# An attention plus mixture-of-experts kernel: expert work in 640-slot blocks with 320-column matmuls, deep gathers, unordered row scatters and a dynamic loop for overflow

## The chip, the cores and the metric

The kernel runs on one core of a Trainium2 chip. The metric is device time in microseconds (us) of one execution; runs of one kernel are summed up by their median. The profile shows one execution, taken by the hardware profiler; its times count from the first instruction. A core has TensorE (PE in the profile; PEld is its weight load), VectorE (DVE), ScalarE (ACT), GpSimd (POOL) and SyncE (SP). SP and POOL also issue transfers; those of POOL go through the software queue q0, those of SP through q1.

## What is computed

Eight batches of eight heads of attention over 576 positions (head width 64) with a position bias made by a small two-layer network; the result, 4608 rows of 512, then passes through a two-layer ReLU network whose weights are chosen by each row's domain:

```python
scores = scale * np.matmul(q, k.transpose(0, 1, 3, 2)) + bias   # bias: position network, per head
attn = softmax(scores); x = np.matmul(attn, v)                  # x: 4608 rows of 512
for e in range(8):
    mask = domain_id == e
    h = np.maximum(x[mask] @ w1[e], 0.0)                        # 512 -> 1024
    out[mask] = h @ w2[e]                                       # 1024 -> 512
```

`domain_id` is drawn at random with a fixed seed. The eight experts get 566, 557, 545, 612, 562, 561, 618 and 587 rows.

## The kernel before

The kernel is written in a tile framework: the author writes operations in program order, and a scheduler at compile time lays them out per engine, taking on each engine the earliest operation of the program that it expects to be ready. Each engine then executes its list strictly in order and waits where an input or a buffer is not there yet. Buffers come from pools; a pool opened after another was closed lies on the same memory, so its first use waits for the last use of the older one. The size of a buffer ring is `bufs`.

The stages, in program order:

1. `_setup_constants` and `_phase_fire` (L47 to L141) build the position bias; `biasall` goes through one long exp on ACT (L141). The buffers of `_phase_fire` (pool `fsb`) are free when its last matmul (L133) is done.
2. `_phase_route` (L144 to L221) gives each row a slot: expert e owns slots 768 e to 768 e + 767 (`CAP` = 768, `NCH` = 6 tiles of 128 slots). DVE computes the position of each row (`posi`, L196), and 36 indirect scatters issued by POOL (L203), each of 128 row numbers, write them into `fire_perm` in device memory, which was filled with -1. All 36 write the same tensor, so each waits for the one before it. Then SP reads the table back (L208), and DVE replaces empty slots by the slot of the same lane in the expert's first tile, giving `gidx` (L221). An empty slot thus repeats a real row.
3. `_phase_attention` (L224 to L320) runs over the batches. POOL loads q and k of a batch with a cast to float16 (L234, L237; ring of 4); per head TensorE transposes them (L247, L250), multiplies (L287), ACT takes the exp (L291, 24 per batch) into `eT` (ring of 8, one per head), DVE multiplies by the bias (L297). SP loads values (L259, L261; ring of 2), POOL casts them into `vext` (L262 to L266; ring of 8). When all heads are there, TensorE multiplies by the values (L308), DVE normalises (L313, L314), and SP stores rows of `fire_x` (L320).
4. `_phase_moe` (L323 to L363) runs over the experts; for each it loads both weight matrices (L329, L332, on POOL with a cast; ring of 2), then for each of 6 tiles of 128 slots: gathers 128 rows of `fire_x` (L336, POOL; ring of 2), transposes them with four TensorE operations (L341), copies to SBUF on DVE (L344), multiplies by w1 in 32 matmuls with 128 columns (L348), applies ReLU on ACT (L353), multiplies by w2 in 8 matmuls with 512 columns (L356), copies the result to SBUF (L359, DVE; ring of 2) and scatters its rows to the output (L360, POOL). All 48 scatters write the output tensor, so each waits for the one before. The pool `msb` of this stage lies on the memory of attention, so its first load (L329) waits for the last store of `fire_x`.

Of the kernel before, what the change touches and what calls it, by code (L numbers as in the profile page):

```python
# [16 lines left out]
P = 128  # L17
# [8 lines left out]
CAP = 768  # L26
NCH = CAP // 128
NTOK = B * S

# [114 lines left out]
def _phase_route(tc, G, moe_domain_id):  # L144
    nc = tc.nc
    perm_dram = nc.dram_tensor("fire_perm", (E * CAP, 1), I32, kind="Internal").ap()
# [18 lines left out]
    ut = pbuf.tile([P, P], F16, tag="ut", name="ut")  # L165
    nc.gpsimd.memset(ut, 1.0)
    nc.gpsimd.affine_select(out=ut, in_=ut, compare_op=AO.is_ge, fill=0.0,
                            base=-1, channel_multiplier=-1, pattern=[[1, P]])
    apref = pbuf.tile([P, 8, 1], F32, tag="apref", name="apref")
    with tc.tile_pool(name="pps", bufs=1, space=bass.MemoryType.PSUM) as pps:  # L170
        app = pps.tile([P, 8], F32, tag="app", name="app")
        nc.tensor.matmul(out=app, lhsT=ut, rhs=rowtot16, start=True, stop=True)
        nc.vector.tensor_copy(out=apref, in_=app.unsqueeze(-1))
    pa = pbuf.tile([P, 8, 80], F32, tag="pa", name="pa")
# [5 lines left out]
    for sh in (1, 2, 4, 8, 16, 32):  # L180
# [6 lines left out]
    etile = pbuf.tile([P, 8, 36], F32, tag="etile", name="etile")  # L187
    nc.vector.tensor_scalar(out=etile, in0=rap(eif, 0, [[1, 8], [0, 36]]),
                            scalar1=float(CAP), scalar2=None, op0=AO.mult)
    nc.vector.tensor_tensor(out=rtile, in0=rtile, in1=etile, op=AO.add)  # L190
# [6 lines left out]
    neg48 = pbuf.tile([P, 48], I32, tag="neg48", name="neg48")  # L197
    nc.gpsimd.memset(neg48, -1)
    nc.sync.dma_start(out=perm_dram.rearrange("(p c) o -> p (c o)", c=48), in_=neg48)
    nidx = pbuf.tile([P, 36], I32, tag="nidx", name="nidx")  # L200
    nc.gpsimd.iota(nidx, base=0, channel_multiplier=1, pattern=[[128, 36]])
    for c in range(36):
        nc.gpsimd.indirect_dma_start(  # L203
            out=perm_dram[:, :],
            out_offset=bass.IndirectOffsetOnAxis(ap=posi[:, c:c + 1], axis=0),
            in_=nidx[:, c:c + 1], in_offset=None)
    permE = pbuf.tile([P, E * NCH, 1], I32, tag="permE", name="permE")
    nc.sync.dma_start(out=permE, in_=bass.AP(tensor=perm_dram.tensor, offset=0,  # L208
                                             ap=[[1, 128], [128, E * NCH], [1, 1]]))
    permEf = pbuf.tile([P, E, NCH], F32, tag="permEf", name="permEf")  # L210
    nc.vector.tensor_copy(out=permEf, in_=permE.rearrange("p (e kk) o -> p e (kk o)", e=E))
    mneg = pbuf.tile([P, E, NCH], F32, tag="mneg", name="mneg")
    nc.vector.tensor_scalar(out=mneg, in0=permEf, scalar1=0.0, scalar2=-1.0,
                            op0=AO.min, op1=AO.mult)
    tsel = pbuf.tile([P, E, NCH], F32, tag="tsel", name="tsel")
    nc.vector.tensor_tensor(out=tsel, in0=permEf[:, :, 0:1].to_broadcast([P, E, NCH]),
                            in1=mneg, op=AO.mult)
    nc.vector.tensor_tensor(out=tsel, in0=tsel, in1=mneg, op=AO.add)
    nc.vector.tensor_tensor(out=permEf, in0=permEf, in1=tsel, op=AO.add)
    G.gidx = pbuf.tile([P, E, NCH], I32, tag="gidx", name="gidx")  # L220
    nc.vector.tensor_copy(out=G.gidx, in_=permEf)  # L221
# [100 lines left out]

def _phase_moe(tc, G, moe_w1, moe_w2, x_dram, out):  # L323
    nc = tc.nc
    with tc.tile_pool(name="msb", bufs=1) as msb, \
         tc.tile_pool(name="mps", bufs=1, space=bass.MemoryType.PSUM) as mps:
        for e in range(E):
            w1e = msb.tile([P, 4, FF], F16, tag="w1e", name="w1e", bufs=2)
            nc.gpsimd.dma_start(out=w1e,  # L329
                                in_=moe_w1[e].rearrange("(dc dl) f -> dl dc f", dl=128))  # L330
            w2e = msb.tile([P, 8, DM], F16, tag="w2e", name="w2e", bufs=2)
            nc.gpsimd.dma_start(out=w2e,  # L332
                                in_=moe_w2[e].rearrange("(fc fl) d2 -> fl fc d2", fl=128))
            for kk in range(NCH):
                xg = msb.tile([P, DM], F16, tag="xg", name="xg", bufs=2)
                nc.gpsimd.indirect_dma_start(  # L336
                    out=xg[:], out_offset=None, in_=x_dram[:],
                    in_offset=bass.IndirectOffsetOnAxis(ap=G.gidx[:, e, kk: kk + 1], axis=0))
                pxt = mps.tile([P, 4, 128], F16, tag="pxt", name="pxt", bufs=2)
                for dc in range(4):  # L340
                    nc.tensor.transpose(out=pxt[:, dc, :],  # L341
                                        in_=xg[:, 128 * dc: 128 * dc + 128], identity=G.idn)
                xgT = msb.tile([P, 4, 128], F16, tag="xgT", name="xgT", bufs=2)
                nc.vector.tensor_copy(out=xgT, in_=pxt)  # L344
                hps = mps.tile([P, FF], F32, tag="hps", name="hps", bufs=2)
                for fc in range(8):
                    for dc in range(4):
                        nc.tensor.matmul(out=hps[:, 128 * fc: 128 * fc + 128],  # L348
# [72 lines left out]
```

## Time and profile before

| what | value |
|---|---|
| runs | 908.75, 915.71, 915.02 us; median 915.02 us |
| span of the profiled execution (its total is not given separately) | 900.5 us |
| granted TensorE clock, mean | 0.935 |
| bias and routing arithmetic | 0 to about 285 us |
| attention | about 285 to 631 us |
| experts | about 632 to 900 us |

The span runs from the first to the last instruction; the measured time of a run also holds what lies before and after. In a row of the timeline stand the start, the duration, the engine, the line and operation, what it writes and reads, how many were merged into the row, and in brackets how long the engine had been idle and what ended that. In a row of waits stand who waited for whom, the total, the number of waits and the longest. In a row of a group stand the total busy time, the mean duration of one in ns, and the idle time of the engine in front of them.

### The profile page before, as it was taken

The page shows a single profiled execution, that of the slowest core. Times are in us where ns is not written, and L with a number is a line of the kernel's source. Part 1 is how long each engine was busy: PE and PEld are TensorE (multiplying, and loading weights), DVE is VectorE, ACT ScalarE, POOL GpSimd, SP SyncE. Part 2 cuts the span into 40 slices and gives each one's busy share as a digit, 9 for nine tenths or more (in the row PEclk, how much of TensorE's full clock was granted, in tenths as well). Part 3 has the DMA queues.
Part 4 walks back from the last instruction along what each step waited for, and adds up shares of the span by engine and source line. Part 5 has one row for each costly group of instructions (what it writes and reads, how often), then busy time and mean ns, then how long its engine had stood idle before and what let it go on. Part 6 is the DMA issues. An engine that isn't in the chain of part 4 may idle for free.

```text
span 900.5 us, 15948 instructions
## 1 busy us (share of the span) xinstructions
PE 573.2 (64%) x6513; PEld 377.7 (42%) x6513; DVE 570.0 (63%) x1106; ACT 259.0 (29%) x279; POOL 290.8 (32%) x547
## 2 busy tenths in 40 slices
PE   0132555555553387786858778786287977887785
PEld 0011233333332245454536555454265655555563
DVE  5989999999999286766758796886021211121121
ACT  0021200000001973535545383754021211211111
POOL 7821100000001735654523243030343453343451
PEclk9999999999999998969879997999599998999999
DMA  1000000000002968389393949020947647736721
GB/s 3 1 5 1 0 1 1 1 1 0 1 1 28 123 55 74 49 99 72 75 59 76 91 59 104 22 61 25 171 125 153 144 120 159 164 98 149 158 99 60
DMA packets 150233, 60.52 MB, mean 67 GB/s; under 512 B 128656, under 2 KB 141456, under 8 KB 150160
## 3 DMA queue, kind: packets, MB, share of 16 engines
q0 software_dynamic: 93824, 45.12, 38.0%
q1 hardware_dynamic: 56336, 14.39, 7.6%
q8 instruction: 51, 0.84, 0.4%
q14 instruction: 22, 0.18, 0.1%
HBM read 68.35 MB, written 17.34 MB: 95 GB/s over the span
## 4 chain that ended last, share of the span: by engine, by line
DVE 31%; DMA 24%; PE 20%; issue 10%; ACT 10%; POOL 4%; POOLq 0%; SPq 0%; DVEq 0%; ACTq 0%
DVE biasall L140 10%; DMA out_dram<-res,gidx 10%; ACT eT L291 8%; DVE hrelu L126 8%; PE sc L287 5%; PE ops L356 5%; DMA fire_x<-xt 4%; PE hps L348 3%; DMA xg<-fire_x,gidx 3%; DMA fire_perm<-nidx,posi 3%; PE hpre L119 3%; PE pu L308 3%; DVE eT L297 3%; DVE WBIG L77 2%; DMA bm<-in_w_dram 2%
## 5 line engine op out<-in xcount | busy, mean ns | idle before, releaser
L291 ACT ACTIVATE eT<-sc 128x1152 f16<-128x1152 f32 (+1 forms) x192 | 172.3, 965 | 138.3 <-PE sc L287 104.2
L359 DVE COPY res<-ops 128x512 f32<-128x512 f32 x48 | 33.2, 692 | 189.7 <-PE ops L356 127.9
L297 DVE TENSOR_TENSOR eT<-eT,biasall 128x576 f16<-128x576 f16 (+1 forms) x320 | 132.1, 459 | 23.9 <-ACT eT L291 22.5
L119 PE MATMUL hpre<-Tnat,WBIG 128*128 128x512 f16 (+1 forms) x288 | 91.7, 422 | 80.9 <-DVE Tnat L99 40.0
L287 PE MATMUL sc<-qkT 128*128 128x512 f16 (+5 forms) x640 | 117.0, 311 | 36.0 <-DVE qkT L255 17.3
L126 DVE TENSOR_SCALAR hrelu<-hpre,b1x 128x576 f16<-128x576 f32 x144 | 113.6, 818 | 2.4 <-PE hpre L119 2.1
L353 ACT ACTIVATE hsb<-hps 128x1024 f16<-128x1024 f32 x48 | 49.1, 1023 | 223.2 <-PE hps L348 192.6
L356 PE MATMUL ops<-w2e,hsb 128*128 128x512 f16 x384 | 98.5, 403 | 17.7 <-ACT hsb L353 9.5
L133 PE MATMUL eb<-W2BIG,hrelu 128*128 128x32 f16 (+1 forms) x720 | 55.0, 197 | 81.6 <-DVE biasall L140 71.8
L348 PE MATMUL hps<-xgT,w1e 128*128 128x128 f16 x1536 | 101.0, 223 | 6.0 <-DVE xgT L344 5.5
L348 PEld LDWEIGHTS <-w1e 128*128 128x128 f16 x1536 | 95.4, 100 | 21.2 <-issue 11.0
L140 DVE CAST biasall<-eb 128x512 f16<-128x512 f32 (+1 forms) x45 | 104.2, 2595 | 0.0
L308 PE MATMUL pu<-vext,eT 128*128 128x65 f16 (+1 forms) x1600 | 77.8, 211 | 27.1 <-DVE xt L314 18.7
L133 PEld LDWEIGHTS <-hrelu 128*128 128x128 f16 (+1 forms) x720 | 46.3, 126 | 110.2 <-issue 91.2
L360 POOL DMA_INDIRECT out_dram<-res,gidx x48 | 47.4, 988 | 131.3 <-DMA out_dram<-res,gidx 71.5
L308 PEld LDWEIGHTS <-eT 128*128 128x128 f16 (+1 forms) x1600 | 68.4, 112 | 39.4 <-DVE xt L314 26.4
L287 PEld LDWEIGHTS <-qkT 128*128 128x128 f16 (+1 forms) x640 | 51.0, 105 | 66.8 <-issue 23.9
L119 PEld LDWEIGHTS <-WBIG 128*128 128x128 f16 x288 | 28.6, 106 | 109.5 <-issue 55.3
L356 PEld LDWEIGHTS <-hsb 128*128 128x128 f16 x384 | 35.7, 102 | 63.3 <-issue 16.7
L231 POOL MEMSET qkT<- 64x1152 f16 x2 | 2.0, 1052 | 180.8 <-PE eb L133 180.8
L262 POOL CAST vext<-vf 128x256 f16<-128x256 f32 x64 | 29.7, 465 | 80.2 <-PE pu L308 64.2
L336 POOL DMA_INDIRECT xg<-fire_x,gidx x48 | 46.8, 975 | 24.7 <-issue 12.9
(78 smaller groups left out, 612.6 us busy)
## 6 DMA issues: line engine op xcount, KB each, us to landing
vf<-in_v_dram SPq DMA_DIRECT2D x64, 128.0 KB
w1e<-in_moe_w_dram POOLq DMA_DIRECT2D x8, 1024.0 KB
w2e<-in_moe_w_dram POOLq DMA_DIRECT2D x8, 1024.0 KB
q<-in_q_dram POOLq DMA_DIRECT2D x8, 576.0 KB
k<-in_k_dram POOLq DMA_DIRECT2D x8, 576.0 KB
fire_x<-xt SPq DMA_DIRECT2D x32, 128.0 KB
vf<-in_v_dram SPq DMA_DIRECT2D x64, 16.0 KB
xg<-fire_x,gidx POOLq DMA_INDIRECT x48
```

The source lines that it names most:

```text
L119: nc.tensor.matmul(out=hp[:, js: js + jwd], lhsT=G.WBIG[:, m, :], rhs=G.Tnat[:, blk, js: js + jwd], start=True, stop=True,)
L126: nc.vector.tensor_scalar(out=hr, in0=hp, scalar1=G.b1x4[:], scalar2=0.0, op0=AO.add, op1=AO.max)
L133: nc.tensor.matmul(out=eb[0:jw, 32 * k16: 32 * k16 + 32], lhsT=hrl[k16][:, j0: j0 + jw], rhs=G.W2BIG[:, 0:32], start=True, stop=True,)
L140: nc.vector.tensor_copy(out=oap, in_=eb[0:jw, :])
L287: nc.tensor.matmul(out=po, lhsT=qkT[:, 1, j0: j0 + jw], rhs=qkT[:, 0, i0s: i0s + iwd], start=True, stop=True)
L291: nc.scalar.activation(out=eT[0:jw0, jgl: jgl + njc, :], in_=sc[0:jw0, 0:njc, :], func=AF.Exp, bias=0.0, scale=scale)
L297: nc.vector.tensor_tensor(out=eT[0:jw, jcn, :], in0=eT[0:jw, jcn, :], in1=G.biasall[0:jw, jcn, h, :], op=AO.mult)
L308: nc.tensor.matmul(out=pu[0:icw, hq, 0:65], lhsT=eTs[h][:, jcn, ic0: ic0 + icw], rhs=vexts[h][:, jcn, 0:65], start=(jcn == 0), stop=(jcn = ...
L348: nc.tensor.matmul(out=hps[:, 128 * fc: 128 * fc + 128], lhsT=w1e[:, dc, 128 * fc: 128 * fc + 128], rhs=xgT[:, dc, :], start=(dc == 0), st ...
L353: nc.scalar.activation(out=hsb, in_=hps, func=AF.Relu, bias=0.0, scale=1.0)
L356: nc.tensor.matmul(out=ops_, lhsT=hsb[:, fc, :], rhs=w2e[:, fc, :], start=(fc == 0), stop=(fc == 7))
L360: nc.gpsimd.indirect_dma_start(out=out[:], out_offset=bass.IndirectOffsetOnAxis(ap=G.gidx[:, e, kk: kk + 1], axis=0), in_=res[:], in_offse ...
```

## The change

- `CAP` goes from 768 to 640, so an expert has 5 tiles. Rows beyond 640 of an expert go to overflow tiles of 128 slots (`NOVF` = 38 of them at most) behind the fixed slots. The routing counts rows per expert with a second small matmul, derives how many overflow tiles there are and which expert each belongs to, and adds an offset to the slots of such rows. This is some 20 more small operations on DVE.
- Empty slots hold `PAD`. The gather index turns them into row 0; the scatter index keeps them, and the scatter skips rows out of bounds.
- The 36 slot scatters and all output scatters are declared free of order among each other (`_no_order`).
- The expert stage works by blocks: five gathers and transposes into `xT`, then the first product over all 640 slots in 8 chunks of two halves with 320 columns (64 matmuls for 160), ReLU per chunk on ACT, then the second product tile by tile. `xg` has a ring of 6, `res` of 4.
- Expert 0's weights are loaded ahead of attention into a pool of their own (`wsb`), which lies between the long-lived pools and attention's, on memory that `_phase_fire` used. Even experts use `wsb`, odd ones `msb`.
- After the last expert a dynamic loop runs once per overflow tile; its count is read from SBUF at run time.

The core of the diff (the arithmetic of the overflow offsets is cut):

```diff
-CAP = 768
+CAP = 640
...
+NOVF = 38
+NSLOT = E * CAP + 128 * NOVF
+PAD = 1 << 20
...
-    ut = pbuf.tile([P, P], F16, tag="ut", name="ut")
+    ut = pbuf.tile([P, 2, P], F16, tag="ut", name="ut")
...
+        for t in range(2):
+            nc.tensor.matmul(out=app[:, t, :], lhsT=ut[:, t, :], rhs=rowtot16, start=True, stop=True)
...
+    cnt = apref[:, 1, :, :]
...
     for c in range(36):
-        nc.gpsimd.indirect_dma_start(
-            out=perm_dram[:, :],
+        _no_order(tc, "slots", nc.gpsimd.indirect_dma_start(
+            out=G.perm_dram[:, :],
             out_offset=bass.IndirectOffsetOnAxis(ap=posi[:, c:c + 1], axis=0),
-            in_=nidx[:, c:c + 1], in_offset=None)
...
+            in_=nidx[:, c:c + 1], in_offset=None))
+    G.sidx = pbuf.tile([P, E * NCH, 1], I32, tag="sidx", name="sidx")
+    nc.sync.dma_start(out=G.sidx, in_=bass.AP(tensor=G.perm_dram.tensor, offset=0,
+                                              ap=[[1, 128], [128, E * NCH], [1, 1]]))
...
+    _pad_to_zero(nc, pbuf, G.gidx, G.sidx, [P, E * NCH, 1], "g")
...
+def _pad_to_zero(nc, pool, out, idx, shape, tag):
+    f = pool.tile(shape, F32, tag="pzf" + tag, name="pzf" + tag)
+    nc.vector.tensor_copy(out=f, in_=idx)
+    ok = pool.tile(shape, F32, tag="pzk" + tag, name="pzk" + tag)
+    nc.vector.tensor_scalar(out=ok, in0=f, scalar1=float(NTOK), scalar2=None, op0=AO.is_lt)
+    nc.vector.tensor_tensor(out=f, in0=f, in1=ok, op=AO.mult)
+    nc.vector.tensor_copy(out=out, in_=f)
...
+def _no_order(tc, key, inst):
+
+    ins = inst.ins if hasattr(inst, "ins") else inst
+    tc.declare_no_dep(ins, group=key, reason="rows of one permutation")
+    tc.add_to_no_dep_group(key, ins)
...
+def _scatter_rows(tc, out, idx, res):
+    _no_order(tc, "out_rows", tc.nc.gpsimd.indirect_dma_start(
+        out=out[:], out_offset=bass.IndirectOffsetOnAxis(ap=idx, axis=0),
+        in_=res[:], in_offset=None, bounds_check=NTOK - 1, oob_is_err=False))
...
+def _load_expert(nc, pool, moe_w1, moe_w2, e):
+    w1e = pool.tile([P, 4, FF], F16, tag="w1e", name="w1e")
+    nc.gpsimd.dma_start(out=w1e, in_=moe_w1[e].rearrange("(dc dl) f -> dl dc f", dl=128))
+    w2e = pool.tile([P, 8, DM], F16, tag="w2e", name="w2e")
+    nc.gpsimd.dma_start(out=w2e, in_=moe_w2[e].rearrange("(fc fl) d2 -> fl fc d2", fl=128))
+    return w1e, w2e
...
+        def gather(idx):
+            xg = msb.tile([P, DM], F16, tag="xg", name="xg", bufs=6)
...
+        def transpose_to(xg, xT):
+            pxt = mps.tile([P, 4, 128], F16, tag="pxt", name="pxt", bufs=2)
...
+            nc.vector.tensor_copy(out=xT, in_=pxt)
+
+        def second(hT, t0, w2e, idx):
+            ops_ = mps.tile([P, DM], F32, tag="ops", name="ops", bufs=2)
+            for fc in range(8):
+                nc.tensor.matmul(out=ops_, lhsT=hT[:, fc, t0: t0 + 128], rhs=w2e[:, fc, :],
+                                 start=(fc == 0), stop=(fc == 7))
+            res = msb.tile([P, DM], F32, tag="res", name="res", bufs=4)
+            nc.vector.tensor_copy(out=res, in_=ops_)
+            _scatter_rows(tc, out, idx, res)
+
         for e in range(E):
...
+            w1e, w2e = G.wts0 if e == 0 else _load_expert(nc, (G.wsb, msb)[e % 2], moe_w1, moe_w2, e)
+            xT = msb.tile([P, 4, CAP], F16, tag="xT", name="xT", bufs=2)
             for kk in range(NCH):
...
+                transpose_to(gather(G.gidx[:, e * NCH + kk, :]), xT[:, :, 128 * kk: 128 * kk + 128])
+            hT = msb.tile([P, 8, CAP], F16, tag="hT", name="hT", bufs=2)
+            for fc in range(8):
+                hps = mps.tile([P, 2, 512], F32, tag="hps", name="hps", bufs=2)
+                for hf in range(2):
+                    for dc in range(4):
+                        nc.tensor.matmul(out=hps[:, hf, 0:HC],
+                                         lhsT=w1e[:, dc, 128 * fc: 128 * fc + 128],
+                                         rhs=xT[:, dc, HC * hf: HC * hf + HC],
+                                         start=(dc == 0), stop=(dc == 3))
+                nc.scalar.activation(out=hT[:, fc, :].rearrange("p (a b) -> p a b", a=2),
+                                     in_=hps[:, :, 0:HC], func=AF.Relu, bias=0.0, scale=1.0)
+            for kk in range(NCH):
+                second(hT, 128 * kk, w2e, G.sidx[:, e * NCH + kk, :])
...
+        novf = nc.values_load(G.novf[0:1, 0:1], min_val=0, max_val=NOVF)
+        with tc.For_i(0, novf, 1) as t:
...
+            w1e, w2e = _load_expert(nc, G.wsb, moe_w1, moe_w2, ex)
...
+            second(hT, 0, w2e, osid[:, 0:1])
...
     _phase_route(tc, G, moe_domain_id)
+    G.wsb = ctx.enter_context(tc.tile_pool(name="wsb", bufs=1))
+    G.wts0 = _load_expert(nc, G.wsb, moe_w1, moe_w2, 0)
     _phase_attention(tc, G, q, k, v, x_dram)
```

The first product has 512 matmuls in all instead of 1536, the second 320 instead of 384, and there are 160 transposes instead of 192.

More of the change, by code (lines that the diff above doesn't have):

```diff
@@ new lines, in _phase_route @@
+    ovc = pbuf.tile([P, 24], F32, tag="ovc", name="ovc")
+    nc.vector.memset(ova, 0.0)
+    nc.vector.memset(ovc, 0.0)
+    nc.vector.tensor_reduce(out=ova[:, 8:16], in_=ovb, axis=AX.X, op=AO.add)
+    ovn = pbuf.tile([P, 8], F32, tag="ovn", name="ovn")
+    nc.vector.tensor_copy(out=ovn, in_=ova[:, 8:16])
+    cur, oth = ova, ovc
+    for sh in (1, 2, 4):
+        nc.vector.tensor_tensor(out=oth[:, 8:16], in0=cur[:, 8:16], in1=cur[:, 8 - sh:16 - sh], op=AO.add)
+        cur, oth = oth, cur
+    incl = pbuf.tile([P, 8, 1], F32, tag="incl", name="incl")
@@ new lines, in gather @@
+        def gather(idx):
+            xg = msb.tile([P, DM], F16, tag="xg", name="xg", bufs=6)
+            nc.gpsimd.indirect_dma_start(
+                out=xg[:], out_offset=None, in_=x_dram[:],
+                in_offset=bass.IndirectOffsetOnAxis(ap=idx, axis=0))
+            return xg
+        def transpose_to(xg, xT):
+            pxt = mps.tile([P, 4, 128], F16, tag="pxt", name="pxt", bufs=2)
+            for dc in range(4):
+                nc.tensor.transpose(out=pxt[:, dc, :],
+                                    in_=xg[:, 128 * dc: 128 * dc + 128], identity=G.idn)
+            nc.vector.tensor_copy(out=xT, in_=pxt)
```

120 lines of the change are left out of this document (59 added, 61 removed).

## The prediction

> **What bounds the kernel now.** I read the page first, then the windows by stage, then the order of time on each engine.
>
> ```profile
> span 900.5 us, 15948 instructions
> PE 573.2 (64%) x6513; PEld 377.7 (42%) x6513; DVE 570.0 (63%) x1106; ACT 259.0 (29%) x279; POOL 290.8 (32%) x547
> ...
> q0 software_dynamic: 93824, 45.12, 38.0%
> ```
>
> No engine is full over the span, so each stage needs its own reading. The bias stage (up to 285 us) is not touched and stays out. The page gives the span but no total for this execution; I set the sum against 900.5 and add 14.5 us, which is the median of the three runs (915.02) less the span. Against the fastest run (908.75) the surround would be 8.3 us.
>
> Expert stage, in windows (columns: busy of PE, weight load, DVE, ACT, POOL, then granted clock, DMA share, GB/s):
>
> ```profile
> 632.00:647.00 15.00, 0.66 (x7) 0.69 (x8) 0.00 (x0) 0.00 (x0) 4.51 (x5) 0.50 1.02 177
> 647.00:895.00 248.00, 203.78 (x2108) 141.10 (x2105) 51.39 (x96) 49.11 (x48) 102.94 (x106) 0.95 0.58 133
> ```
>
> TensorE is 82% busy for 248 us, every other engine has room, and before that stand 15 us in which only DMA works. This stage is TensorE with gaps: 48 tiles in 248 us is 5.17 us a tile. What ends its gaps:
>
> ```profile
> POOL out_dram L360 <- DMA out_dram<-res,gidx: 71.5, 20, 7.3
> ...
> DVE res L359 <- DMA out_dram<-res,gidx: 59.7, 12, 6.7
> ...
> PE pxt L341 <- DMA xg<-fire_x,gidx: 37.6, 7, 17.6
> ```
>
> Each row scatter waits for the landing of the one before it, DVE waits for a result buffer to come free, and TensorE then waits for gathers that stand behind the scatters on POOL.
>
> Attention stage: ACT's first exp of a batch (24 to a batch) comes at
>
> ```profile
> 309.61 2.65 ACT L291 ACTIVATE eT<-sc 128x1152 f16<-128x1152 f32 x3
> 481.71 2.67 ACT L291 ACTIVATE eT<-sc 128x1152 f16<-128x1152 f32 x3 [11.89 <-PE sc L287]
> 631.96 0.77 POOL L329 DMA_DIRECT2D w1e<-in_moe_w_dram  x1 [29.40 <-DMA fire_x<-xt]
> ```
>
> The first four batches take (481.71 - 309.61) / 4 = 43.0 us each, the last four, up to the release of the expert weights, (631.96 - 481.71) / 4 = 37.6. The slow four are those among which the 36 slot scatters stand:
>
> ```profile
> 287.48 1.98 POOL L234 DMA_DIRECT2D q<-in_q_dram  x1
> 294.44 1.04 POOL L203 DMA_INDIRECT fire_perm<-nidx,posi  x1 [4.98 <-DVE posi L196]
> 295.50 1.81 POOL L237 DMA_DIRECT2D k<-in_k_dram  x1
> 297.61 0.99 POOL L203 DMA_INDIRECT fire_perm<-nidx,posi  x1 [0.30 <-issue]
> 298.64 0.40 POOL L262 CAST vext<-vf 128x256 f16<-128x256 f32 x1
> ...
> POOL fire_perm L203 <- DMA fire_perm<-nidx,posi: 40.4, 19, 6.2
> 452.60 0.37 SPq L208 DMA_DIRECT2D permE<-fire_perm  x1
> ```
>
> POOL takes a scatter as soon as its predecessor is expected to have landed, and fills the time between with q, k and value casts; the chain runs from 294 to 452 us, 158 / 36 = 4.4 us a scatter.
>
> **Part 1, 640 slots for 768.** The drawn tokens per expert are 545 to 618, so no expert needs a sixth tile and the overflow loop runs zero times. 48 tiles become 40, and 8 scatters and 8 gathers go.
>
> **Part 2, one expert as a block.** Durations of dense TensorE work:
>
> ```profile
> 678.59 1.68 PE L356 MATMUL ops<-w2e,hsb 128*128 128x512 f16 x7 [0.23 <-issue]
> 884.02 1.90 PE L356 MATMUL ops<-w2e,hsb 128*128 128x512 f16 x8
> 654.44 0.61 PE L341 MATMUL pxt<-idn,xg 128*128 128x128 f16 x8
> 655.35 0.38 PE L348 MATMUL hps<-xgT,w1e 128*128 128x128 f16 x4 [0.29 <-DVE xgT L344]
> ```
>
> Eight take 0.22 us more than seven: 0.22 us per matmul of 512 columns, 0.1375 for 320 columns if it goes by columns (bounds: 0.11, half of the longer one, and 0.22, all of it). An expert: 64 x 0.1375 = 8.8 us for the first product, 40 x 0.22 = 8.8 for the second, 20 transposes x 0.076 = 1.5, in all 19.1 us. Two gaps remain. The first product needs five transposed tiles through two PSUM buffers. The rows show 0.91 us from the first transpose of a pair to the first matmul; two and a half pairs are 2.3 us, of which 1.5 is TensorE's own work, and a result copy of 0.69 us can stand in front of it on DVE: 0.8 to 1.5 us, I take 1.2. Between the products nothing: ACT needs about 0.69 us for 640 columns (between its 1023 ns for 1024 columns and 639 for 576; rows below), TensorE 1.1 us for the next chunk, and there are two chunk buffers. Without that second buffer it would be 0.7 us a chunk, 45 us in all. At the granted 0.95 to 0.97 of this stage 20.3 becomes 21.0 us an expert. Eight experts: 168 us. Bounds: 19.1 with no gap (153 us), and today's 5.17 us a tile for 40 tiles (207 us). I take 168, nearer the dense rows, since the three waits above lose their cause in parts 3 and 4: 248 - 168 = -80 us.
>
> ```profile
> L359 DVE COPY res<-ops 128x512 f32<-128x512 f32 x48 | 33.2, 692 | 189.7 <-PE ops L356 127.9 <-DMA out_dram<-res,gidx 59.7 <-issue 2.1
> L291 ACT ACTIVATE eT<-sc 64x576 f16<-64x576 f32 x64 | 40.9, 639 | 3.5 <-PE sc L287 3.5
> L353 ACT ACTIVATE hsb<-hps 128x1024 f16<-128x1024 f32 x48 | 49.1, 1023 | 223.2 <-PE hps L348 192.6 <-DMA w1e<-in_moe_w_dram 30.6
> ```
>
> [...]
>
> **Part 3, scatters without order, four result buffers.** The wait on the previous landing goes. What is late next is a scatter that stands behind a weight load:
>
> ```profile
> 664.68 2.26 DMA out_dram<-res,gidx
> ...
> 677.62 8.12 DMA out_dram<-res,gidx
> ```
>
> 2.3 us alone, 8.1 behind a load. An expert's five results come 1.76 us apart; four buffers and two PSUM banks hold 6 x 1.76 = 10.6 us, more than 8.1. So nothing on the path. DMA has to carry it: share 0.58 over 248 us is 144 us, 3.0 a tile; 40 tiles at the same weight traffic stay under that, 144 / 168 = 0.86. That cover is thin; a rival prices it.
>
> **Part 4, expert 0's weights early and gathers six deep.** Now the first gather stands behind two weight loads:
>
> ```profile
> 633.92 1.06 POOL L336 DMA_INDIRECT xg<-fire_x,gidx  x1 [0.30 <-issue]
> 635.28 0.99 POOL L336 DMA_INDIRECT xg<-fire_x,gidx  x1 [0.30 <-issue]
> 646.35 1.01 PE L341 MATMUL pxt<-idn,xg 128*128 128x128 f16 x8 [17.60 <-DMA xg<-fire_x,gidx]
> 647.50 4.08 PE L348 MATMUL hps<-xgT,w1e 128*128 128x128 f16 x49
> ...
> 783.93 4.29 DMA xg<-fire_x,gidx
> ```
>
> After: five gathers 1.3 us apart from about 632.5, the last landing some 3 us on (between the 2.3 of a scatter and the 4.3 of a gather among loads): 632.5 + 4 x 1.3 + 1 + 3 = 641.7. The first product starts there and not at 647.5: -6 us (bounds -10, 0).
>
> What it costs: the load of 4 MB goes to POOL when the bias buffers come free, in front of q of batch 0. Two issues are 1.7 us, and the loads delay what is behind them in the queue by about the 12 us that the gather above waited. q is used 8.3 us after its issue (287.48), k 8 us after that, and the first scores follow:
>
> ```profile
> 295.78 0.68 PE L247 MATMUL ptq<-idn,q 64*64 64x64 f16 x9 [6.64 <-DMA q<-in_q_dram]
> 305.10 2.08 PE L287 MATMUL sc<-qkT 128*128 128x512 f16 x8 [0.15 <-issue]
> ```
>
> With 12 us more in front of q and k right behind it, not after a scatter, the first scores come near 312 instead of 305, and ACT takes its first one only at 309.61 anyway: +3 us.
>
> **Part 5, the slot scatters without order.** All 36 are ready at one time, and each counts as earlier in the program than the value casts: they stand on POOL as a block, 36 x 1.3 us (issue plus the 0.3 gap) = 47 us.
>
> ```profile
> L193 DVE TENSOR_REDUCE posf<-rtile 128x36 f32<-128x288 f32 x1 | 0.7, 659 | 0.0
> 340.70 3.50 PE pu L308 x60
> 349.07 0.40 POOL L262 CAST vext<-vf 128x256 f16<-128x256 f32 x1
> 364.67 0.64 POOL L262 CAST vext<-vf 128x256 f16<-128x256 f32 x1
> 351.64 2.67 ACT L291 ACTIVATE eT<-sc 128x1152 f16<-128x1152 f32 x3 [16.47 <-issue]
> ```
>
> The added routing arithmetic on DVE (about 20 operations of at most 0.7 us) delays its start by some 5 us to about 300, by which time k of batch 0 is out. The casts for batch 0 begin at 347 and take up to 16 us (the eight heads of the next batch: 349.07 to 364.67 with scatters between), so its products with the values, which started at 340.70, end near 366, and batch 1 starts there, not at 351.64 (+14). The index load waits on SP behind the scatters, with value loads queued behind it; that falls in the same block. From then on no scatter stands in the way: seven batches at 37.6 end at 366 + 263 = 629. Against 631.96 that is -3; with a few us for scatters stuck behind q and k loads in the full queue I take +2 for the stage, part 4's +3 included. Bounds: no block at all, 312.5 + 8 x 37.6 = 613 (-19); block before k of batch 0, scores start after 355, +27.
>
> **Part 6, the loop that runs zero times.** [...] No row shows one. The nearest are the end of the kernel, where the last scatter's issue at 895.48 to the span's end takes 5.0 us; bounds 0 and 15 (three such ends), I take 5, one end.
>
> ```profile
> 895.48 0.96 POOL L360 DMA_INDIRECT out_dram<-res,gidx  x1 [2.95 <-DVE res L359]
> ```
>
> **Sum.** 900.5 + 2 (attention) - 6 (start) - 80 (experts) + 5 (loop) = 821.5; plus 14.5 = **836 us**.
>
> **The rivals.**
> *The slot scatters block earlier or longer*, ahead of k or waiting for room in the queue: for it speaks that POOL already now takes them first; against, the later start. Attention +27: 861 us.
> *They spread well*, because POOL interleaves them as now: -19 instead of +2: 815 us.
> *DMA binds the experts*: 0.86 share leaves little, and bursts of a weight load with five scatters stall DVE, which then holds up the next transposes. At 24.5 us an expert, +28: 864 us.
> [...]
> *Slower*: the scatters stand in a block but each still costs its landing, 4.4 us as now, through a limit on transfers in flight. The block is then 158 us, casts of batch 0 start near 458, batch 1 near 477 instead of 352 (+125), less 16 saved in batches 1 to 3: 836 - 2 + 109 = 943 us. It decides from about 3.5 us a scatter. Against it: two gathers in a row issue 1.3 us apart without waiting for a landing (rows of part 4).
> *The loop does run*: the counts exclude it; one pass would cost about 30 us (15.5 from the load's issue to the first product, 631.96 to 647.50, a tile of 5.2 and two ends of 5).
>
> **How the numbers follow.** Forecast 0.47 (its own range 820 to 850); earlier block 0.15; spread 0.15; DMA-bound 0.10; full clock 0.08; slower 0.04; loop runs 0.01. A measurement of this kernel tells about 1% from no change. Only the slower case and, for a hair, combinations of the costly ones reach 906: faster 0.94, same 0.02, slower 0.04. The range takes in all cases but the slow one, with combinations of the two good and of two bad ones cut off: 803 to 872.
>
> **What would show it.** Right: first-product matmuls of 0.14 us, 20 to 22 us between experts, no wait of POOL or DVE on a scatter, TensorE over 90% busy in the expert stage, first expert matmul some 10 us after the last attention store; 36 slot scatters in one stretch of about 47 us, batch 1 starting near 366, later batches every 37 to 38 us; under 10 us from last result to end. Wrong: value casts after 370, expert periods over 24 us with DVE waiting on scatters, or more than 10 us at the loop.

## The result and the profile after

The kernel after takes **875.86 us** (median of 4 runs, 875.14 to 876.13) against 912.75 us for the kernel before beside it (908.75 to 915.71). The ratio is 0.9609, 95% interval 0.9553 to 0.9665: faster, but 40 us short of the 836 forecast and outside its range. The profiled execution took 875.14 us, its span is 873.2.

The stages are cut at the same events as in the prediction. From the timeline after: ACT's first exp, the first gather (in this text "the release" of the experts), the first expert product, the last result copy, and the last output scatter.

```profile
360.02 2.73 ACT L347 ACTIVATE eT<-sc 128x1152 f16<-128x1152 f32 x3 [49.41 <-PE sc L343]
682.16 1.07 POOL L408 DMA_INDIRECT xg<-fire_x,gidx  x1 [29.27 <-DMA fire_x<-xt]
690.86 4.47 PE L439 MATMUL hps<-xT,w1e 128*128 128x320 f16 x16
864.59 0.69 DVE L426 COPY res<-ops 128x512 f32<-128x512 f32 x1 [1.04 <-PE ops L423]
868.34 0.98 POOL L387 DMA_INDIRECT out_dram<-res,sidx  x1 [3.52 <-issue]
```

| stage | before, us | after, us | change | predicted |
|---|---|---|---|---|
| start to release of the experts | 631.96 | 682.16 | +50.2 | +2 |
| release to first expert product | 15.5 | 8.7 | -6.8 | -6 |
| eight experts, to the end of the last result copy | 247.7 | 174.4 | -73.3 | -80 |
| from there to the span's end (with the loop) | 5.3 | 7.9 | +2.6 | +5 |
| span | 900.5 | 873.2 | -27.3 | -79 |
| around the span | not shown | 1.9 | | 14.5, carried over |

For before, 895.2 is the end of its last result copy (timeline of DVE):

```profile
894.51 0.69 DVE L359 COPY res<-ops 128x512 f32<-128x512 f32 x1 [3.22 <-PE ops L356]
```

The experts gave nearly what was forecast; attention ate two thirds of it. The whole 50 us is there before the first exp: it came at 309.61 and now comes at 360.02, and from it to the release both kernels take 322 us. What GpSimd does ahead of it (timeline of POOL, last row PE):

```profile
286.64 0.99 POOL L394 DMA_DIRECT2D w1e<-in_moe_w_dram  x1 [181.00 <-PE eb L136]
290.61 1.76 POOL L290 DMA_DIRECT2D q<-in_q_dram  x1
301.38 1.06 POOL L259 DMA_INDIRECT fire_perm<-nidx,posi  x1 [9.01 <-DVE posi L252]
302.74 1.01 POOL L259 DMA_INDIRECT fire_perm<-nidx,posi  x1 [0.30 <-issue]
...
345.73 0.96 POOL L259 DMA_INDIRECT fire_perm<-nidx,posi  x1 [0.30 <-issue]
346.69 1.82 POOL L293 DMA_DIRECT2D k<-in_k_dram  x1
357.55 0.69 PE L306 MATMUL ptk<-idn,k 64*64 64x64 f16 x9 [51.12 <-DMA k<-in_k_dram]
```

q of batch 0 is out at 292.37. POOL then stands 9 us for the slot numbers (posi), although k, which needs none of them, is the next load; then it issues all 36 scatters, one each 1.26 us, and k only after the last. TensorE waits for that one load, and ScalarE for TensorE. Among the waits from 285 to 400 us TensorE has one row of that size, and VectorE has one:

```profile
PE ptk L306 <- DMA k<-in_k_dram: 51.1, 1, 51.1
DVE pzfg L273 <- DMA sidx<-fire_perm: 49.9, 1, 49.9
```

The second row is VectorE at the index table: SyncE's read of it (sidx) needs all scatters, and VectorE, which takes its instructions in order, stands at the first operation on it. Here the two waits cover one another. The two causes can't be told apart from this trace alone; the experiments do that.

In the expert stage (windows; columns as before) TensorE is busy for 90% in place of 82%:

```profile
690.00:865.00 175.00, 157.73 (x976) 93.51 (x976) 40.73 (x76) 45.07 (x64) 83.24 (x87) 0.95 0.78 163
```

### The profile page after: what moved, and what is told of

Read it like the earlier page. It is cut to its first block, busy times and chain, and to the rows that moved or that the text cites. A ratio compares the mean times of both kernels' runs of the same rounds, so it can differ in the third digit from the quotient of the medians.

```text
span 873.2 us, 13744 instructions
## 1 busy us (share of the span) xinstructions
PE 540.9 (62%) x5394; PEld 334.4 (38%) x5394; DVE 567.8 (65%) x1110; ACT 256.0 (29%) x295; POOL 270.3 (31%) x533
## 4 chain that ended last, share of the span: by engine, by line
DVE 33%; PE 24%; DMA 12%; issue 12%; ACT 10%; POOL 7%; POOLq 0%; SPq 0%; DVEq 0%
DVE biasall L143 11%; ACT eT L347 10%; PE sc L343 9%; DVE hrelu L129 7%; DMA fire_x<-xt 4%; DMA out_dram<-res,sidx 4%; PE hps L439 4%; POOL fire_perm L259 4%; PE hpre L122 3%; PE pu L364 3%; DVE WBIG L80 3%; DVE eT L353 3%; POOL xg L408 2%; DMA bm<-in_w_dram 2%; PE ops L423 2%
## 5 line engine op out<-in xcount | busy, mean ns | idle before, releaser
L343 PE MATMUL sc<-qkT 128*128 128x512 f16 (+5 forms) x640 | 126.9, 331 | 30.3 <-DVE qkT L311 17.4
L426 DVE COPY res<-ops 128x512 f32<-128x512 f32 x40 | 27.7, 692 | 131.1 <-PE ops L423 114.5
L443 ACT ACTIVATE hT<-hps 128x640 f16<-128x640 f32 x64 | 45.1, 704 | 141.9 <-PE hps L439 141.9
L439 PE MATMUL hps<-xT,w1e 128*128 128x320 f16 x512 | 78.5, 318 | 0.0
L423 PE MATMUL ops<-w2e,hT 128*128 128x512 f16 x320 | 70.4, 379 | 0.0
L394 POOL DMA_DIRECT2D w1e<-in_moe_w_dram x8 | 6.8, 846 | 204.2 <-PE eb L136 181.0
L306 PE MATMUL ptk<-idn,k 64*64 64x64 f16 x576 | 34.9, 208 | 54.7 <-DMA k<-in_k_dram 51.1
L439 PEld LDWEIGHTS <-w1e 128*128 128x128 f16 x512 | 52.9, 104 | 23.5
L387 POOL DMA_INDIRECT out_dram<-res,sidx x40 | 39.9, 997 | 59.5 <-DVE res L426 55.7
L306 PEld LDWEIGHTS <-k 64*64 64x64 f16 x576 | 27.9, 121 | 71.0 <-DMA k<-in_k_dram 51.3
```

The lines of the kernel that those rows point to most:

```text
L306: nc.tensor.transpose(out=ptk[:, 64 * m: 64 * m + 64], in_=k16[0:64, g9, :], identity=G.idn[0:64, 0:64])
L343: nc.tensor.matmul(out=po, lhsT=qkT[:, 1, j0: j0 + jw], rhs=qkT[:, 0, i0s: i0s + iwd], start=True, stop=True)
L423: nc.tensor.matmul(out=ops_, lhsT=hT[:, fc, t0: t0 + 128], rhs=w2e[:, fc, :], start=(fc == 0), stop=(fc == 7))
L439: nc.tensor.matmul(out=hps[:, hf, 0:HC], lhsT=w1e[:, dc, 128 * fc: 128 * fc + 128], rhs=xT[:, dc, HC * hf: HC * hf + HC], start=(dc == 0), ...
L443: nc.scalar.activation(out=hT[:, fc, :].rearrange("p (a b) -> p a b", a=2), in_=hps[:, :, 0:HC], func=AF.Relu, bias=0.0, scale=1.0)
```

## The experiments

Theory A: the block of unordered slot scatters stands on POOL ahead of k of batch 0, and attention starts late by its length. Theory A2: the index table, put on VectorE's list too early, adds a wait of its own. Rival B: the early weight loads in front of q make the start late. Rival C, the prediction's own reading: ordered scatters cost each of the first four batches about 5.4 us, so that removing their order pays in attention. Ratios are to the kernel before, with 95% intervals.

**The order of the slot scatters put back in the kernel after, and taken away in the kernel before.**

```diff
 # e1_slots_ordered: after, with
-        _no_order(tc, "slots", nc.gpsimd.indirect_dma_start(
+        nc.gpsimd.indirect_dma_start(
 # b1_before_unordered: before, with the reverse
```

> The changed kernel (875.9 us) with one part undone: the 36 slot scatters wait for each other again, as before. Theory A (the block of 36 scatters on GpSimd in front of k of batch 0 costs the start of attention 45 to 50 us): first exp of batch 0 comes near 313 instead of 360, the time falls to 825 to 835 us. Theory B (the late start comes from expert 0's weights in front of q and from the longer routing arithmetic, the scatters were only in the way by chance): first exp stays later than 340, time above 855. Beside it: if scatters among the batches cost 5.4 us a batch, as the prediction read it, batches 0 to 3 take 43 us and 4 to 7 take 37 to 38; if not, all take the 40 us that they take in the changed kernel.

> The kernel before with one part of the change alone: its 36 slot scatters declared free of order. In its program they then stand as one block between q and k of batch 0. Theory A: first exp about 40 us later than 309.6, and no gain later: 950 us (ratio 1.04). If scatters among the batches cost 5.4 us a batch, 22 us of it come back: 930 us. Theory B: 910 us or less.

Measured: after with ordered slot scatters 841.44 us, 0.9293 (0.9215 to 0.9372), 34 us below the kernel after (29 by the ratios, since the kernel before beside it ran 7 us quicker); before with unordered ones 940.95 us, 1.0355 (1.0261 to 1.0449), slower than before. One edit, both signs, in both kernels. In the first the second scatter has to wait for the first to land, and k goes out in that gap (timeline of POOL, e1_slots_ordered):

```profile
301.06 1.06 POOL L259 DMA_INDIRECT fire_perm<-nidx,posi  x1 [9.01 <-DVE posi L252]
302.13 1.80 POOL L293 DMA_DIRECT2D k<-in_k_dram  x1
305.93 1.04 POOL L259 DMA_INDIRECT fire_perm<-nidx,posi  x1 [2.00 <-DMA fire_perm<-nidx,posi]
```

In the second k stands at the end of the block (timeline of POOL, b1_before_unordered):

```profile
294.97 1.04 POOL L203 DMA_INDIRECT fire_perm<-nidx,posi  x1 [4.97 <-DVE posi L196]
...
339.30 0.96 POOL L203 DMA_INDIRECT fire_perm<-nidx,posi  x1 [0.30 <-issue]
340.25 1.82 POOL L237 DMA_DIRECT2D k<-in_k_dram  x1
```

The first exp comes at 313.2 us and at 355.4. In e1_slots_ordered the weights of expert 0 are still loaded in front of q, and 313.2 is 3.6 us later than before: that, and not 50, is the price of rival B (the weights and the longer routing arithmetic together), near the +3 of the prediction. Theory A holds for the late start.

The whole times were missed (825 to 835 was expected, and 950, or 930 by rival C). Attention behind the first exp also changed: up to the release it takes 340 us in e1_slots_ordered against 322 in the kernel after, and 317 in b1_before_unordered against 322 before. So taking the order away gives back 6 us of attention in the kernel before, and not the 22 that rival C's 5.4 us a batch would; the 18 us of e1_slots_ordered come up again with the clock below.

**The loads put ahead of the block, and the scatters written six at a time behind batches 0 to 5.**

```diff
 # e2_loads_first
+        first = [load_qk(b) for b in range(2)]
+        _route_scatter(tc, G, 0, 36)
+        _route_index(tc, G)
         for b in range(B):
+            q16, k16 = first[b] if b < 2 else load_qk(b)
 # e3_spread, at the end of the loop over batches
+            if b < 6:
+                _route_scatter(tc, G, 6 * b, 6 * b + 6)
+            if b == 5:
+                _route_index(tc, G)
```

> The changed kernel with q and k of batches 0 and 1 put in front of the scatters in the program, the scatters still one block without order. This is the order that the prediction assumed. By its steps: first exp near 312, value casts from about 347, batch 1 starts near 366 instead of 400, end of attention some 34 us earlier, 840 us. Theory A the same within 8 us. Theory B (weights in front of q): first exp after 340 and 860 us or more. If DVE's wait for the index table is what holds batch 0 (a third reading: it is 50 us long in the changed kernel), the gain is under 10 us.

> The changed kernel with the scatters issued six at a time behind the code of batches 0 to 5, still without order, and the index table read after the last: the scheduler then fills gaps of GpSimd between value casts with them. Theory A: no block, first exp near 312, attention 48 us shorter, 825 us. If the batches then run at the 37.6 us that the last four took before: 808 us. Theory B: above 855.

Measured: 862.72 us, 0.9531 (0.9464 to 0.9598), and 847.7 us, 0.9344 (0.9266 to 0.9422). Both start attention at 313, yet neither gains the full 47 us. In e2_loads_first the block and VectorE's wait for the index are still there, so it is k, and not the index, that held back the first exp. In it batch 0 lasts 81.4 us; in e3_spread batch 1 lasts 60.8. The waits of VectorE from 300 to 400 us, in e2_loads_first:

```profile
DVE pzfg L285 <- DMA sidx<-fire_perm: 28.8, 1, 28.8
```

and in e3_spread, where the read is written behind batch 5 in the program and VectorE still got the operation in batch 1:

```profile
DVE pzfg L285 <- DMA sidx<-fire_perm: 25.0, 1, 25.0
```

So the wait of theory A2 is there without the late k, hidden behind k in the kernel after, and the place of a line in the program doesn't set the place on the engine. The same goes for the scatters: those of e3_spread were not spread over six batches, POOL issued twelve from 301 to 330 us and the other 24 from 349.8 to 388.5, all before batch 2 began. Whether the wait costs time is the next question.

**The index read held back** until batch 5's last result tile exists, in the spread kernel and in the one with its loads first.

```diff
 # e10_spread_late_index (on e3), e13_loads_first_late_index (on e2)
     G.sidx = pbuf.tile([P, E * NCH, 1], I32, tag="sidx", name="sidx")
+    nc.vector.tensor_copy(out=G.sidx[0:64, 0, :], in_=late[0:64, 0, 0:1])
```

> The scatters go out six behind each of batches 0 to 5, as in e3_spread, and the read of the index table (SyncE's load of sidx, and VectorE's four operations on it) is held back until batch 5's last result tile exists, by a one-column VectorE write from that tile into sidx. Theory (VectorE, which takes its instructions in order, stood 24.98 us behind the index table in batch 1 of e3_spread): the wait is gone, batch 1 falls from 60.8 to about 40 us, attention ends near 630 and the time is about 825 us, 20 below e3_spread's. Rival (the wait only stood beside other lateness, for instance SyncE's value loads or the casts): batch 1 stays above 50 us and the time stays at 845.

> e2_loads_first (q and k of batches 0 and 1 issued ahead of the block of 36 scatters) with the index read held back until batch 5. It puts the order that the prediction assumed, block behind k of batch 0 and no wait for the index. If the 28.81 us that VectorE waited for the index table in e2_loads_first were the rest of the miss, batch 1 starts near 366 as predicted and the time is about 835. If the value casts behind the block set it (they began at 358.48 in e2_loads_first, eight pairs of them are needed before batch 0 can be finished): batch 1 starts near 390 to 395 all the same and the time stays near 860.

Measured: e10 839.19 us, 0.9204 (0.9139 to 0.9270). The wait is gone and batch 1 takes 41.1 us, 20 less, so there it did cost time. But batches 5 and 6 took 44.5 and 47.6 (39.2 and 38.1 in e3_spread), and the whole is 8.5 us below e3_spread in place of 20; against the expected 825, 14 us are missing. What these batches have in common comes with the next experiment. e13 865.53 us, 0.9522 (0.9474 to 0.9570): no gain over e2. Its wait for the index is gone too, and batch 1 still starts only at 385.9, not at 366; the rival was right, so in e2_loads_first other work of the same length covered the index wait. This kernel has k of batch 0 ahead of the block, as the prediction assumed (and q and k of batch 1 too), and shows what that order costs (timelines of POOL, PE and ACT, e13):

```profile
354.59 0.40 POOL L337 CAST vext<-vf 128x256 f16<-128x256 f32 x1
355.27 0.38 PE L383 MATMUL pu<-vext,eT 128*128 128x65 f16 x4 [13.21 <-POOL vext L339]
...
365.58 0.38 PE L383 MATMUL pu<-vext,eT 128*128 128x65 f16 x4 [3.92 <-POOL vext L337]
...
372.62 0.38 PE L383 MATMUL pu<-vext,eT 128*128 128x65 f16 x4 [2.74 <-POOL vext L337]
...
385.87 2.15 ACT L366 ACTIVATE eT<-sc 128x1152 f16<-128x1152 f32 x2 [42.95 <-PE sc L362]
```

The casts start at 354.59, when the block ends. There are two buffers for loaded values, so the heads come two at a time, each pair after a new load, the last cast of values starting at 373.45; then batch 0's remaining products and batch 1's transposes and scores take until 385.9.

**Six buffers for the attention result**, in the kernel after and in e10.

```diff
 # e8_xt6 (on after), e11_late_index_xt6 (on e10)
-                xti = asb.tile([P, 8, D], F16, tag="xt", name="xt", bufs=2)
+                xti = asb.tile([P, 8, D], F16, tag="xt", name="xt", bufs=6)
```

> The kernel after with six buffers in place of two for xt, and nothing else. If the pauses for the store bring the half clock: 8 to 12 us below the kernel after (about 865). If not: 876. On either side the block of 36 scatters stays ahead of k, so the first exp stays at 360 and attention cannot end before about 660.

> e10_spread_late_index with six buffers in place of two for the result tile xt. Theory (the half-clock stretches begin where TensorE pauses at a batch's end, because VectorE waits for a store to free xt): the pauses of about 2 us at the batch ends go, half-clock time in attention falls below 40 us, the batches take about 37.5 us each, and the time is 10 to 15 us below e10_spread_late_index. Rival (the half-clock stretches come from the run of small matmuls at a batch's end, whatever the store does): same batches and the same time as e10_spread_late_index within 4 us.

Measured: e8 855.01 us, 0.9411 (0.9336 to 0.9487), 21 us below the kernel after (18 by the ratios); e11 818.55 us, 0.8992 (0.8937 to 0.9047), 21 below e10, beside which it ran. Both are more than was expected, and somewhat more than VectorE had waited for stores of xt in the attention of the kernel after (waits of DVE, 360 to 682 us):

```profile
DVE xt L370 <- DMA fire_x<-xt: 16.2, 8, 3.0
```

Windows over attention, after and then e8 (of the last three numbers the first is the granted clock; in the clock records of the kernels before and after it is 1 or 0.5, and a window shows the mean):

```profile
360.00:682.00 322.00, 254.39 (x3361) 171.39 (x3359) 238.72 (x661) 173.28 (x192) 86.44 (x318) 0.84 0.74 69
```

```profile
360.00:660.00 300.00, 244.18 (x3362) 164.40 (x3359) 237.30 (x661) 173.25 (x192) 90.22 (x319) 0.90 0.79 74
```

The same matmuls take 10 us less of TensorE's time, and the clock was halved less: 61 us at half clock in place of 102. How much of the gain is the pause and how much the clock, the runs don't separate. Nor is it shown that the pauses for the store bring the half clock: in e11 it was expected to fall below 40 us and is 85 (115 in e10), one batch of e8 has 31 us of it without any such wait, and the three kernels below that share the attention of the kernel after have 90 to 143. A close view of the batch end at 436 us in the kernel after (windows):

```profile
432.00:436.50 4.50, 3.25 (x89) 2.94 (x89) 3.64 (x13) 0.00 (x0) 2.04 (x13) 1.00 0.29 86
436.50:453.50 17.00, 16.83 (x129) 9.19 (x130) 12.12 (x30) 10.38 (x11) 5.97 (x27) 0.50 0.30 68
453.50:476.00 22.50, 16.01 (x239) 11.49 (x238) 15.54 (x45) 11.61 (x14) 3.51 (x2) 0.88 0.90 71
```

TensorE has short pauses at the batch end (72% busy), and then 17 us at half clock while it is 99% busy. What ends the half clock these rows don't show.

This also bears on rival C. Take the 97 batches 1 to 7 of all fourteen profiles (without e3's batch with the index wait): a batch takes 35.9 us plus 0.32 us for each us at half clock, with a correlation of 0.93 and 1.0 us of scatter around that line. A line through such points doesn't say which of the two makes the other. The kernel before's batches 1 to 3, which I put down to slot scatters, had 13.7, 17.1 and 13.7 us at half clock against 3.4 to 8.6 in its last four, and stand above the line by 2.2, 1.9 and 4.3 us. So of the 5.8 us by which they were longer (43.4 against 37.6) about half, 2.8 us, may be the scatters' and the other half goes with the clock. The two order edits bear that out: with the order put back (e1) batches 1 to 3 stand 1.8, 0.5 and 3.5 us above the line, and in the kernel before without it (b1) they stand within 0.3 us of it. Batches 5 and 6 of e10 fit the same line (27.4 and 35.2 us at half clock).

**Which part carried the experts.** Slots, order and the ring of gather buffers (xg) undone one at a time in the kernel after, and ten result buffers (res) put into e11.

```diff
 # e5_cap768
-CAP = 640
+CAP = 768
 # e6_out_ordered
-    _no_order(tc, "out_rows", tc.nc.gpsimd.indirect_dma_start(
+    tc.nc.gpsimd.indirect_dma_start(
 # e7_ring2
-            xg = msb.tile([P, DM], F16, tag="xg", name="xg", bufs=6)
+            xg = msb.tile([P, DM], F16, tag="xg", name="xg", bufs=2)
 # e12_late_index_xt6_res10 (on e11)
-            res = msb.tile([P, DM], F32, tag="res", name="res", bufs=4)
+            res = msb.tile([P, DM], F32, tag="res", name="res", bufs=10)
```

> The kernel after with 768 slots an expert in place of 640: blocks of 2 x 384 columns, six gathers, six scatters an expert. It keeps blocks, unordered scatters and deep gathers and gives back the slots alone. Theory (TensorE binds an expert, so its time goes by its columns): 21.7 x 6/5 = 26.0 us an expert, the expert stage 226 us in place of 191. Rival (gathers and scatters bind): below 23 or above 28 us an expert. Read by the stage, since the attention ahead of it moves the whole.

> The kernel after with its output scatters ordered again, each waiting for the one before. Theory (an ordered scatter is held until the last one has landed, about 5.2 us each by the 31 us that six took per expert in the kernel before): five of them take 26 us an expert, more than the 21.7 of TensorE, and the expert stage is about 225 us. Rival (order was never the limit in the kernel before, its small matmuls were): the stage stays within 4 us of 191.

> The kernel after with two gather buffers (xg) in place of six. Theory (of the prediction: deep gathers pay at the first expert alone): the first expert product comes about 8 us later than the 8.7 us after release of the kernel after, since the third to fifth gather wait for a buffer, later experts stay at 21.7 us; the expert stage is about 199 us. Rival (the transposes stand at the end of each expert, so the gathers beyond two are exposed for every expert, two rounds of about 7 us): 14 us an expert more, the stage near 300.

> e11_late_index_xt6 with ten result buffers (res) in place of four. The prediction held that with four buffers nothing waits for an output scatter. In the kernel after the fifth result copy of an expert waits for the first scatter of that expert to land (2.80 us at 712.68, 2.57 us at 733.94; six such waits, 16.6 us in all), and TensorE's transposes of the next expert stand behind it. Theory (those waits are on the path): the waits go, the expert stage falls from 191.2 to 178 to 184 us, the time from 818.6 to about 808. Rival (they stand beside gathers that are late anyway): the stage stays at 191.

One run each for the first three, read by the stage from release to end, which is 190.4 to 192.5 us wherever the experts are those of the kernel after, and 268.5 before:

| kernel | whole, us | stage, us | from expert to expert, us |
|---|---|---|---|
| after | 875.86 | 191.0 | 22.2 |
| e5_cap768 | 900.32 | 218.9 | 25.2 |
| e6_out_ordered | 924.64 | 231.9 | 26.9 |
| e7_ring2 | 959.15 | 268.5 | 31.8 |
| e12_late_index_xt6_res10 | 803.75 | 175.8 | 20.0 |

(The last column is from ACT's first relu of the first expert to that of the eighth, by seven.) Undoing the slots costs 28 us, near the 35 expected, and undoing the order 41, near 34. Undoing the ring of six costs 77.5, all that the stage gained; 8 was expected, and 109 by the rival written down with it (gathers late at every expert), which was right in kind. Together they come to 146 of a gain of 77.5, so the costs overlap, and undoing one at a time doesn't split the gain. The products by blocks of 320 columns were not undone by any run. e7's waits of TensorE from 700 to 945 us and its window:

```profile
PE pxt L416 <- DMA xg<-fire_x,gidx: 70.4, 15, 11.3
```

```profile
700.00:945.00 245.00, 169.24 (x968) 97.58 (x969) 40.43 (x75) 45.05 (x64) 81.52 (x85) 0.81 0.53 110
```

With two buffers the third to fifth gathers of an expert can't go before its first transposes; the transposes stand between the experts, and the clock is lower on top (0.81 against 0.95).

The result buffers: in the kernel after the copies of an expert's results run 1.72 us apart until the fifth, which has to wait for a scatter (timeline of DVE, after):

```profile
704.01 0.69 DVE L426 COPY res<-ops 128x512 f32<-128x512 f32 x1 [12.48 <-PE ops L423]
...
709.19 0.69 DVE L426 COPY res<-ops 128x512 f32<-128x512 f32 x1 [1.04 <-PE ops L423]
712.68 0.69 DVE L426 COPY res<-ops 128x512 f32<-128x512 f32 x1 [2.80 <-DMA out_dram<-res,sidx]
713.29 2.21 DVE L418 COPY xT<-pxt 128x512 f16<-128x512 f16 x5
```

The xT copies of the next expert stand behind it on VectorE, and TensorE's first product behind those. With ten buffers no such wait is left, and in the window of the stage (e12) TensorE is busy for 95% at clock 0.98:

```profile
632.00:793.00 161.00, 152.74 (x976) 91.21 (x976) 41.01 (x76) 45.04 (x64) 83.34 (x86) 0.98 0.84 178
```

The stage fell by 15 us, more than the 7 to 13 expected. e12 is the best kernel of the study: 803.75 us (800.07 to 809.14), 0.8827 of the kernel before (0.8757 to 0.8898), against 0.9609 for the change as it was made.

## Why the prediction was right or wrong

- *Part 1 (slots, loop never entered)*: right; 40 output scatters in the trace, and 28 us when the slots are given back.
- *Part 2 (21.0 us an expert, eight for 168)*: right in its main term, 174.4 measured. The dense sum of 19.1 and the 1.2 us gap stand: in e12 TensorE is busy for 152.74 / 8 = 19.1 us an expert and goes from one to the next in 20.0.
- *Part 3 ("So nothing on the path")*: this step failed. The waits cost 15 us by e12; 8 of them were covered, because 21.0 us an expert was forecast where 20.0 is reached without the waits, and 7 show. It set the four buffers and two PSUM banks (10.6 us) against a landing of 8.1. The banks let TensorE run on (its 40 matmuls of the second product go from 702.08 to 710.88 without a wait), but not VectorE, which stands at the fifth copy with the next expert's xT copies behind it; buffers alone are four copies, 4 x 1.72 = 6.9 us, and the first scatter's buffer came free 8.7 us after the first copy began (704.01 to 712.68).
- *Part 4 (start -6, cost +3)*: right: -6.8, and 3.6 late for the first exp in e1. What it didn't price is the ring of six at the experts after the first; part 2 had that in its sum only as waits that "lose their cause".
- *Part 5 (the slot scatters as a block of 47 us from about 300, +2)*: it was missed by 48 us: batch 1 started at 399.8 and not at 366 (34 us), the seven batches behind took 282 us and not 263 (19), and 5 of that was in the sum as a reserve (for scatters in a full queue, which the kernel after doesn't show: each of the 36 but the first goes out 0.30 or 0.31 us behind the one before it). The block was right, 301.38 to 346.69, and so was its reason. The step that failed is "**by which time k of batch 0 is out**". k is a separate issue on the same engine, and it stood behind the block, as the quoted rows of before could have told: there too the first scatter goes ahead of k (294.44 and 295.50), and k followed only because the second scatter had to wait for a landing. Without order that opening is gone. This is the rival "ahead of k", given 0.15; its price of 27 us was half of the 50 measured, because it let the batches behind the block run at 37.6 us each, where they took 40.3.
- That pace is the second failed step, for the 19 us. "The slow four are those among which the 36 slot scatters stand" told about half of it: they are also the batches with more half clock. Behind the block, with no scatter among them, the batches took 38.3 to 43.4 us, and attention from its first exp took 322 us as before.
- A third error lay behind it, unseen in this result: "so its products with the values, which started at 340.70, end near 366, and batch 1 starts there". In e13, which has k ahead, batch 1 starts at 385.9. Of these 20 us, 8 are the later start of the casts (354.6, not 347), to which the loads of batch 1 ahead of the block add in e13; from the first cast to batch 1 it takes 31 us and not 19, since the casts come in four rounds of two loads and more work follows the last. So even with k ahead part 5 was about 12 us short.
- *Part 6 (loop +5)*: 2.6 us for all that lies behind the last result; its last scatter stands 3.5 us for no wait that the profile shows. The 5 us were taken from the kernel's end; what a loop of no turns costs alone, no run shows. The step is small and in its bounds.
- *The 14.5 us around the span*: wrong by 12.6. In this profile it is 1.9 us, 1.5 to 2.0 in the others, and 1.7 to 1.9 in all runs of the kernel before beside the experiments. The profiled execution of before, with its span of 900.5, thus took about 902 us, less than the 909 to 916 of the runs, and the median less the span mixed two executions. For the same reason the stages above sum to 27 us of gain where the medians show 37.

The errors add up: 836 + 48.2 (attention) - 0.8 (start) + 6.7 (experts) - 2.4 (tail) - 12.6 (around) = 875.1.

Of the other rivals, the slower one is excluded: a scatter without order takes 1.26 us. The scatters did not spread, they stood in one block, and the loop did not run (40 output scatters). DMA didn't bind the experts: its share was 0.78, and 0.84 at 20 us an expert. The full clock, to which the chances give 0.08, was not there (0.95 in the expert stage); e12 came near it (0.98).

## What to carry to other kernels

Taking an order away also takes away the gaps through which other work on the same in-order queue went out: before pricing it, list what stands behind the released instructions on that engine, above all a load that the next stage needs first, and put that load ahead of them, or keep the order (841 us here, against 863 with the loads ahead). Look as well at who reads their result, because an in-order engine that gets that read too early stands still for the whole stretch (VectorE for 28.8 us in e2_loads_first). A buffer ring is priced by what stands behind the waiting instruction on its own engine, not only by whether its producer can run on (ten result buffers for four took 15 us off the expert stage in e12).

## What the runs showed of the hardware

Unordered scatters of 128 row numbers issue every 1.26 us (0.96 and a gap of 0.30) for 36 in a row in the kernel after; with order they came every 4.4 us on average in the kernel before. Over 97 batches a batch is 0.32 us longer for each us at half clock. In the clock records of the kernels before and after, the 38 stretches at half clock that don't run into the end of the record lasted 3.41, 6.83, 10.24, 17.07 or 20.48 us; one batch of e10 had 35.2 us of half clock. In the kernel after, pauses of 0.4 to 2.2 us at two batch ends were followed by 17 and 20.5 us of it. With six result buffers in place of two (e8) attention had 61 us at half clock in place of 102, and took 300 us in place of 322; what part of that the pauses themselves held is not shown.
